# Each K and V load of a decode kernel issued as two transfers of 64 partitions

## The chip, the cores and the metric

The kernel runs on one core of one Trainium2 chip. The metric is the device time of one execution in microseconds; lower is better. The core has five engines that matter here: TensorE (PE in the profile, with its weight loads shown apart as PEld), VectorE (DVE), ScalarE (ACT), GpSimd (POOL) and SyncE (SP). SP computes nothing in this kernel: it issues every DMA. The profile counts sixteen DMA engines, which carry the data of all loads from HBM into SBUF.

## The reference

Four sequences, one token each, go through attention and a SwiGLU feed-forward layer, twice, with the same weights and the same K and V cache both times:

```python
B, Sq, D = 4, 1, 448
Hq, Hkv, Sk, Dh = 16, 8, 8192, 256
W = min(4096, max(256, Sk // 4))                     # 2048
q = (x @ wq).reshape(B, Sq, Hq, Dh).transpose(0, 2, 1, 3)
k = jnp.repeat(k_cache[:, :, Sk - W:, :], 2, axis=1)
v = jnp.repeat(v_cache[:, :, Sk - W:, :], 2, axis=1)
p = softmax(einsum("bhqd,bhkd->bhqk", q, k) * Dh ** -0.5)
A = einsum("bhqk,bhkd->bhqd", p, v).transpose(0, 2, 1, 3).reshape(B, Sq, Hq * Dh) @ wo
Bf = (silu(x @ w_gate) * (x @ w_up)) @ w_down
x = x + A(layernorm(x)); x = x + Bf(layernorm(x))    # twice over
```

Everything is bfloat16. The window of one sequence and one K/V head is 2048 rows of 256 values, so 1 MB of K and 1 MB of V. There are 4 x 8 such pairs in a layer.

## The kernel before, in words

**The unit of work is a pair**, one sequence t and one K/V head. For each pair the window of K is loaded as two transfers of 512 KB (line 609), the window of V as two more (line 626). Each goes into one buffer `half<i>` of 128 partitions x 4 KB; there are 15 such buffers (`NPOOL`). Each partition of a K load gets one run of 4096 bytes from HBM; each partition of a V load gets two runs of 2048 bytes.

**What uses a load.** A K load waits for one VectorE transposition (line 617), which writes it into one of six `KT` buffers and so frees the `half` buffer. Two of them make the pair's K ready for 32 matmuls that make the scores (line 637). Then come the row maximum, the exponentials on ScalarE (line 656), a rearrangement, and two groups of eight matmuls with V (line 677), one group for each V load. A V buffer is free when its group is done. After that the pair's two heads are normalised, flipped, and go through the output projection (line 724) with the weights in `wo_sb`.

**What is loaded once.** The weights (`wq_sb`, `wo_sb`, `wg_sb`, `wu_sb`, `wd_sb`, by line 389) are loaded once. Of each sequence the last five heads of K (transposed) and of V are kept from the first layer for the second (`KEEP_K`, `KEEP_V`). So 64 pairs are computed, and 44 of them load K and V: 88 loads of each.

**The order.** The program first builds a graph of operations with ranks, then a planner (`Graph.schedule`) lays the operations out on five queues by rank and by estimated times, and takes for each K or V load the buffer that is free first. What comes out is one fixed order for each engine. All DMAs stand in SP's order. A load that reuses a buffer waits on SP for the last reader of that buffer; whatever stands behind it on SP waits too. Each buffer has its own semaphore, `h<i>`. A load adds 16 to it when it has landed, and its readers wait for the count (`Graph._count`, `Graph.emit`).

**The planner's estimates of a load** are its bytes and the length of its runs (`o.nbytes`, `o.run`), not the number of DMA instructions.

Of the kernel before, what the change touches and what calls it, by code (L numbers as in the profile page):

```python
# [32 lines left out]
KLEAD = 2.2  # L33
VLAG = 1.3
# [20 lines left out]

class Op:
    __slots__ = ("i", "eng", "dur", "rank", "emit", "deps", "succ", "nbytes", "dsem", "dval",
                 "start", "end", "pos", "waits", "inc", "val", "known", "run", "cell", "rel")

    def __init__(self, i, eng, dur, rank, emit):  # L60
        self.i, self.eng, self.dur, self.rank, self.emit = i, eng, dur, rank, emit
        self.deps = {}
        self.succ = []
        self.nbytes = 0
        self.dsem = None
        self.dval = 0
        self.cell = None
        self.rel = ()
        self.inc = False
        self.val = 0  # L70
        self.waits = []


class Graph:
# [12 lines left out]
    def op(self, eng, dur, rank, emit, r=(), w=(), bank=(), acc=()):  # L87

        o = Op(len(self.ops), eng, dur, rank, emit)
        self.ops.append(o)  # L90
        for k in r:
            d = self.writer.get(k)
            if d is not None:
                self._dep(o, d, d.eng != eng or eng != PE)
        for k in tuple(w) + tuple(acc):
            for d in self.readers.get(k, ()):
                self._dep(o, d, d.eng != eng or eng != PE)
            d = self.writer.get(k)
            if d is not None:
                self._dep(o, d, d.eng != eng or eng != PE)  # L100
        for b in bank:
            last = self.banks.setdefault(b, {})
            for e, d in last.items():
                if e != eng:
                    self._dep(o, d, True)
            last[eng] = o
        for k in r:
            self.readers.setdefault(k, []).append(o)
        for k in tuple(w) + tuple(acc):
            self.writer[k] = o  # L110
            self.readers[k] = []
        return o

    def dma(self, rank, nbytes, emit, sem, r=(), w=(), run=8192, cell=None):

        o = self.op(SP, 0.05, rank, emit, r=r, w=w)
        o.run = run
        o.nbytes = nbytes
        o.cell = cell
        if cell is None:  # L120
            self._count(o, sem)
        return o

    def _count(self, o, sem):
        o.dsem = sem
        self.dcount[sem] = self.dcount.get(sem, 0) + 16
        o.dval = self.dcount[sem]


# [98 lines left out]
    def emit(self, eng_name, eng, sems, dsems):  # L228
        for o in self.order[eng_name]:
            for d in o.waits:  # L230
                if d.dsem is not None:
                    eng.wait_ge(dsems[d.dsem], d.dval)
                else:
                    eng.wait_ge(sems[d.eng], d.val)
            ins = o.emit(eng)
            if o.dsem is not None:
                ins.then_inc(dsems[o.dsem], 16)
            elif o.inc:
                ins.then_inc(sems[eng_name], 1)

# [38 lines left out]
def build(nc, A_x, A_k_cache, A_v_cache, A_wq, A_wo, B_x, B_w_gate, B_w_up, B_w_down, out):  # L279
    s0 = A_k_cache.shape[2] - WIN  # L280
    g = Graph()

    with ExitStack() as es:
        def sb(name, shape, dt):
            return es.enter_context(nc.sbuf_tensor(name, shape, dt))
# [6 lines left out]
        half = [sb(f"half{s}", [128, 8 * DH], BF16) for s in range(NPOOL)]  # L292
# [70 lines left out]
        for a in range(4):  # L363
            g.op(DVE, 0.1, R0, lambda e, a=a: e.memset(qmask[32 * a:32 * a + 32, a:a + 1], DH ** -0.5), r=("qmask",),
                 w=(f"qmask{a}",))
        g.op(DVE, 0.2, R0, lambda e: e.tensor_copy(
            permb[:, :].rearrange("p (r l) -> p r l", l=4), identb[:, :].rearrange("p (l r) -> p r l", l=4)),
            r=("identb",), w=("permb",))
        for a in range(4):
# [5 lines left out]
            w=("osel",))  # L375
        g.op(DVE, 0.2, R0, lambda e: e.tensor_reduce(lomask[:, :], iv[:, :, 1, :], AX.XY, ALU.add), r=("identb",),
             w=("lomask",))
# [199 lines left out]
        def x_in(e):  # L577
            last = None
            for cc in range(4):
# [6 lines left out]
             r=("z",), w=tuple(f"x{t}" for t in range(B)), bank=("Z",))  # L586
# [11 lines left out]
        pos = -1  # L598

        def pair(pos, si, side, nside, t, layer, kvh):  # L600
            p_, s_, q_ = pos % NY, pos % NS, pos % NQ
            if layer == 1 and (t, kvh) in kt_held:
                ks = kt_held.pop((t, kvh))
            else:
                ks = kt_free.pop(0)
                ksrc = A_k_cache[t, kvh, s0:s0 + WIN, :].rearrange("(p j) d -> p (j d)", p=128)
                for hf in range(2):
                    cell = []
                    g.dma(pos - KLEAD, 1 << 19, lambda e, cell=cell, hf=hf: e.dma_start(  # L609
                        half[cell[0]][:, :], ksrc[:, 2048 * hf:2048 * hf + 2048]), None, w=(f"k{pos}_{hf}",), run=4096,  # L610
                        cell=cell)
                    for q in range(TRP):
                        def tr(e, cell=cell, hf=hf, q=q):
                            n = 2 // TRP
                            src = half[cell[0]][:, :].bitcast(UINT32).rearrange("p (l k s) -> p l k s", l=2, k=16)
                            dst = KT[ks][:, :].bitcast(UINT32).rearrange("p (k l r) -> p l k r", k=16, l=4)
                            return e.transpose(dst[:, 2 * hf + q * n:2 * hf + q * n + n], src[:, q * n:q * n + n])  # L617
                        o = g.op(DVE, 1.12 / TRP + 0.06, pos, tr, r=(f"k{pos}_{hf}",), w=(f"kt{ks}_{hf}_{q}",))
                    o.rel = (cell,)
            if layer == 1 and (t, kvh) in v_held:  # L620
                vs = v_held.pop((t, kvh))
            else:
                vsrc = A_v_cache[t, kvh, s0:s0 + WIN, :].rearrange("(a q g) d -> q a g d", a=4, q=128)
                vs = [[], []]
                for hv, cell in enumerate(vs):
                    g.dma(pos + VLAG, 1 << 19, lambda e, cell=cell, hv=hv: e.dma_start(  # L626
                        half[cell[0]][:, :].rearrange("p (a g d) -> p a g d", a=2, g=4),
                        vsrc[:, 2 * hv:2 * hv + 2, :, :]), None, w=(f"v{t}_{kvh}_{hv}",), run=2048, cell=cell)
            at = first[t].index(kvh)
            keep_k, keep_v = (layer == 0 and at >= HKV - k for k in (KEEP_K, KEEP_V))  # L630

            def scores(e):
# [11 lines left out]
                r=(f"qc{t}_{kvh}",) + tuple(f"qmask{a}" for a in range(4)), w=(f"qe{q_}",))  # L644
# [3 lines left out]
                r=(f"s{s_}",), w=(f"pmax{s_}",), bank=(f"S{s_}",))  # L648
# [5 lines left out]
                r=(f"m{s_}",), w=(f"negm{s_}",), bank=(f"S{s_}",))  # L654
            for n in range(2):
# [3 lines left out]
                    r=(f"s{s_}", f"negm{s_}"), w=(f"praw{s_}_{n}",), bank=(f"S{s_}",))  # L659
            g.op(PE, 0.03, pos, lambda e: e.matmul(Yb[p_][:, 64:96], lhsT=permb[:, :], rhs=praw[s_][:, :], start=True,  # L660
                                                   stop=False, skip_group_check=True),
                 r=(f"praw{s_}_0", f"praw{s_}_1", "permb"), w=(f"yp{p_}",), bank=(f"Y{p_}",))
            g.op(PE, 0.03, pos, lambda e: e.matmul(Yb[p_][:, 32:64], lhsT=onesb[:, :], rhs=praw[s_][:, :], start=False,  # L663
                                                   stop=False, skip_group_check=True),
                 r=(f"praw{s_}_0", f"praw{s_}_1", "onesb"), w=(f"ysum{p_}",), bank=(f"Y{p_}",))
# [5 lines left out]
                r=(f"ysum{p_}",), w=(f"rs{p_}",), bank=(f"Y{p_}",))  # L671

            def pv(e, hv):
                last = None
                for a in range(2):
                    for gg in range(4):
                        last = e.matmul(Yb[p_][32 * gg:32 * gg + 4, 256:512],  # L677
                                        lhsT=pT[p_][:, 4 * gg + 2 * hv + a, :, :].rearrange("p y n -> p (y n)"),
                                        rhs=half[vs[hv][0]][:, 1024 * a + 256 * gg:1024 * a + 256 * gg + 256], start=False, stop=False, skip_group_check=True)
                return last  # L680
            for hv in range(2):
                kw = dict(acc=(f"y{p_}",)) if hv else dict(w=(f"y{p_}",))
                o = g.op(PE, 0.385, pos, lambda e, hv=hv: pv(e, hv), r=(f"pT{p_}", f"v{t}_{kvh}_{hv}"),
                         bank=(f"Y{p_}",), **kw)
                if not keep_v:
# [4 lines left out]
                 w=(f"oh{p_}",), bank=(f"Y{p_}",))  # L690
# [4 lines left out]
            def flip(e):  # L695
# [9 lines left out]
                r=(f"yo{p_}", f"ri{p_}"), w=(f"oT{si % 2}_{side}",), bank=(f"Y{p_}",))  # L705
# [26 lines left out]
        for si, pairs in enumerate(steps()):  # L732
# [8 lines left out]
            for t, layer in full:  # L741
                pos_ = pos
                pos = pos_ - CROSS
# [12 lines left out]
                pos = pos_  # L756
# [5 lines left out]
        dsems = {d: es.enter_context(nc.semaphore(f"d_{d}")) for d in g.dcount}  # L762
# [60 lines left out]
```

## Time and profile before

| | before |
|---|---|
| three runs | 323.88, 326.10, 326.27 us; median 326.1 us |
| profiled execution, from first to last instruction (span) | 322.9 us |
| what the median has beyond that span | 3.2 us |
| moved by DMA | 105.27 MB, mean 326 GB/s |
| busy: PE / DVE / POOL / ACT | 72% / 60% / 26% / 22% |
| K and V loads | 88 + 88, 512 KB each |
| granted TensorE clock | 1.000 |

The profile has no time of its own for the profiled execution beside its span; the runs lie 1.0 to 3.4 us above that span.

How to read it. A row of the groups of instructions names the line of the kernel, the engine, the operation and the tiles (output, then inputs), the shape and the count; then the busy time and the mean of one, and the idle time of that engine just before, with what ended most of it. A row of the chain of waits is one piece of the work that ended last: its start, its length, and what it was. A "DMA" piece there runs from the issue of a transfer to its landing. SPq rows are DMA instructions on SP's queue; a long one was held up at the queue. In a table of windows, each row gives for a stretch of time the busy time of each engine (with the number of instructions), the granted clock, the mean busy share of the sixteen DMA engines, and the rate in GB/s. The share is made from packet times and can come out a few per cent over 1.

### The profile page before, as it was taken

The page shows a single profiled execution, that of the slowest core. Times are in us where ns is not written, and L with a number is a line of the kernel's source. Part 1 is how long each engine was busy: PE and PEld are TensorE (multiplying, and loading weights), DVE is VectorE, ACT ScalarE, POOL GpSimd, SP SyncE. Part 2 cuts the span into 40 slices and gives each one's busy share as a digit, 9 for nine tenths or more (in the row PEclk, how much of TensorE's full clock was granted, in tenths as well). Part 3 has the DMA queues.
Part 4 walks back from the last instruction along what each step waited for, and adds up shares of the span by engine and source line. Part 5 has one row for each costly group of instructions (what it writes and reads, how often), then busy time and mean ns, then how long its engine had stood idle before and what let it go on. Part 6 is the DMA issues. An engine that isn't in the chain of part 4 may idle for free.

```text
span 322.9 us, 12873 instructions
## 1 busy us (share of the span) xinstructions
PE 232.6 (72%) x5728; PEld 169.7 (53%) x5728; DVE 192.6 (60%) x608; ACT 72.4 (22%) x289; POOL 84.9 (26%) x199
## 2 busy tenths in 40 slices
PE   3654454446588788578796895679787959889875
PEld 2542322234476465366664653567555636686554
DVE  5386555652145778765447787855377874656332
ACT  1112111111022333211231322113223322123310
POOL 3312111112023223240233331313233413134221
DMA  7999999999999999999889999999899999748000
GB/s 277 399 407 392 393 396 397 391 396 397 391 362 308 338 368 346 400 362 309 301 272 373 375 351 405 355 365 339 277 359 377 357 386 391 277 140 305 5 0 5
DMA packets 42327, 105.27 MB, mean 326 GB/s; under 512 B 3096, under 2 KB 7200, under 8 KB 41888
## 3 DMA queue, kind: packets, MB, share of 16 engines
q1 hardware_dynamic: 42272, 104.45, 88.0%
q8 instruction: 45, 0.74, 0.9%
q14 instruction: 10, 0.08, 0.1%
HBM read 104.44 MB, written 0.00 MB: 323 GB/s over the span
## 4 chain that ended last, share of the span: by engine, by line
DMA 38%; PE 34%; DVE 12%; SPq 7%; issue 5%; ACT 2%; POOL 0%; DVEq 0%
DMA half<-in_A_k_cache_dram 20%; DMA half<-in_A_v_cache_dram 12%; PE Y L677 11%; PE S L637 8%; DVE KT L617 6%; DMA wd_sb<-in_B_w_down_dram 5%; PE Z L473 4%; SPq L389 4%; PE A L724 3%; PE Z L514 3%; DVE oh L691 2%; PE Z L542 2%; SPq L609 2%; DVE small L652 2%; SPq L626 1%
## 5 line engine op out<-in xcount | busy, mean ns | idle before, releaser
L617 DVE STREAM_TRANSPOSE KT<-half 128x1024 uint32<-128x1024 uint32 x88 | 108.3, 1233 | 13.3 <-DMA half<-in_A_k_cache_dram 12.9
L637 PE MATMUL S<-qe,KT 128*128 128x8 bf16 x2048 | 64.6, 168 | 22.4 <-DVE KT L617 18.5
L677 PE MATMUL Y<-half,pT 128*4 128x256 bf16 x1024 | 70.0, 403 | 9.6 <-DMA half<-in_A_v_cache_dram 8.7
L637 PEld LDWEIGHTS S<-qe,KT 128*128 128x128 bf16 x2048 | 59.7, 104 | 30.7 <-DVE KT L617 20.8
L687 POOL TENSOR_TENSOR small<-small 128x2 f32<-128x2 f32 x64 | 44.3, 696 | 113.5 <-DVE small L669 103.3
L656 ACT ACTIVATE praw<-S,small 128x16 bf16<-128x16 f32 x128 | 28.7, 279 | 84.6 <-DVE small L652 83.9
L691 DVE SCALAR_TENSOR_TENSOR oh<-oh,small,Y 128x256 bf16<-128x256 bf16 x64 | 30.1, 472 | 23.9 <-ACT oh L689 23.4
L689 ACT ACTIVATE oh<-Y 128x256 bf16<-128x256 f32 x64 | 24.6, 384 | 74.2 <-PE Y L677 74.2
L641 POOL TENSOR_TENSOR qe<-qc,qmask 128x64 bf16<-128x64 bf16 x64 | 18.6, 294 | 71.3 <-PE S L637 52.3
L677 PEld LDWEIGHTS Y<-half,pT 128*4 128x4 bf16 x1024 | 20.0, 94 | 21.8 <-DMA half<-in_A_v_cache_dram 11.5
L646 DVE TRANSPOSE_TENSOR_REDUCE pmax<-S 128x1 bf16<-128x32 f32 x64 | 13.4, 211 | 27.1 <-PE S L637 25.3
L724 PE MATMUL A<-oT,wo_sb 128*128 128x1 bf16 (+1 forms) x688 | 24.8, 166 | 6.4 <-DVE oT L702 6.1
L724 PEld LDWEIGHTS A<-oT,wo_sb 128*128 128x128 bf16 x688 | 22.2, 105 | 10.5 <-DVE oT L702 8.5
L697 PE MATMUL Y<-osel,oh 128*128 128x2 bf16 x128 | 13.3, 173 | 17.4 <-DVE oh L691 17.2
L652 DVE TENSOR_REDUCE small<-S 128x2 f32<-128x128 f32 x64 | 17.4, 282 | 10.4 <-PE S L649 8.3
L666 ACT ACTIVATE pT<-Y 128x64 bf16<-128x64 f32 x64 | 14.1, 222 | 40.7 <-PE Y L663 40.4
L697 PEld LDWEIGHTS Y<-osel,oh 128*128 128x128 bf16 x128 | 8.8, 111 | 27.0 <-DVE oh L691 24.5
L649 PE MATMUL S<-identb,pmax 128*128 128x128 bf16 x64 | 16.6, 284 | 4.5 <-DVE pmax L646 3.6
L473 PE MATMUL Z<-xn,wq_sb 128*128 128x1 bf16 (+1 forms) x480 | 15.6, 165 | 2.6 <-DMA wq_sb<-in_A_wq_dram 1.9
L473 PEld LDWEIGHTS Z<-xn,wq_sb 128*128 128x128 bf16 x480 | 14.3, 104 | 3.4 <-DMA wq_sb<-in_A_wq_dram 2.0
L669 DVE TENSOR_REDUCE small<-Y 128x2 f32<-128x32 f32 x64 | 11.0, 177 | 7.1 <-ACT pT L666 6.8
L440 POOL TENSOR_SCALAR st<-st 128x1 f32<-128x1 f32 x16 | 4.3, 267 | 41.2 <-DVE st L428 40.7
(76 smaller groups left out, 212.0 us busy)
## 6 DMA issues: line engine op xcount, KB each, us to landing
half<-in_A_k_cache_dram SPq DMA_DIRECT2D x88, 512.0 KB, 7.0
half<-in_A_v_cache_dram SPq DMA_DIRECT2D x88, 512.0 KB, 6.7
wo_sb<-in_A_wo_dram SPq DMA_DIRECT2D x8, 448.0 KB, 12.3
wq_sb<-in_A_wq_dram SPq DMA_DIRECT2D x3, 1024.0 KB, 6.9
wd_sb<-in_B_w_down_dram SPq DMA_DIRECT2D x1, 1568.0 KB, 16.3
wg_sb<-in_B_w_gate_dram SPq DMA_DIRECT2D x1, 1344.0 KB, 14.2
wu_sb<-in_B_w_up_dram SPq DMA_DIRECT2D x1, 1344.0 KB, 14.7
wq_sb<-in_A_wq_dram SPq DMA_DIRECT2D x1, 512.0 KB, 10.4
```

The lines of the kernel that those rows point to most:

```text
L473: last = e.matmul(o, lhsT=lhsT, rhs=rhs, start=(cc == 0 and hh == 0 and ee == 0), stop=(cc == 3), skip_group_check=True)
L617: return e.transpose(dst[:, 2 * hf + q * n:2 * hf + q * n + n], src[:, q * n:q * n + n])
L637: last = e.matmul(Sb[s_][:, 8 * gg:8 * gg + 8], lhsT=kt[:, gg, ce // 2, ce % 2, :], rhs=qe[q_][:, ce, :, :], start=(gg == 0 and ce == 0), ...
L641: g.op(POOL, 0.25, pos - SLEAD - 1, lambda e: e.tensor_tensor(qe[q_][:, :, :, :], qc[t][:, kvh, :, :].unsqueeze(2).broadcast_to([128, 8, 4 ...
L652: g.op(DVE, 0.2, pos, lambda e: e.tensor_reduce(negm[s_][:, :], Sb[s_][:, 128:256].rearrange("p (k n) -> p n k", n=2), AX.X, ALU.max, nega ...
L656: g.op(SCA, 0.17, pos, lambda e, n=n: e.activation(praw[s_][:, :].rearrange("p (k n) -> p n k", n=2)[:, n, :], Sb[s_][:, 0:32].rearrange(" ...
L677: last = e.matmul(Yb[p_][32 * gg:32 * gg + 4, 256:512], lhsT=pT[p_][:, 4 * gg + 2 * hv + a, :, :].rearrange("p y n -> p (y n)"), rhs=half[ ...
L687: g.op(POOL, 0.25, pos, lambda e: e.tensor_tensor(ri[p_][:, :], rs[p_][:, :], expo[:, 1:3], op=ALU.pow), r=(f"rs{p_}", "expo"), w=(f"ri{p_ ...
L689: g.op(SCA, 0.28, pos, lambda e: e.activation(oh[p_][:, :], Yb[p_][:, 256:512], ACT.Copy), r=(f"y{p_}",), w=(f"oh{p_}",), bank=(f"Y{p_}",))
L691: g.op(DVE, 0.4, pos, lambda e: e.scalar_tensor_tensor(out=oh[p_][:, :], in0=oh[p_][:, :], scalar=lomask[:, 0:1], in1=Yb[p_][:, 256:512], ...
L697: last = e.matmul(Yb[p_][:, 2 * dh:2 * dh + 2], lhsT=oh[p_][:, :].rearrange("p (m e) -> p e m", e=2)[:, dh, :], rhs=osel[:, :], start=Fals ...
L724: last = e.matmul(Av[:, cc, sl], lhsT=wo_sb[:, 4 * kvh + k, c0:c0 + 128], rhs=oT[si % 2][:, k % 2, k // 2, 0:n], start=False, stop=False, ...
```

## The change

Each load of K or V is issued as two DMA instructions, one for partitions 0 to 63 and one for partitions 64 to 127, one right behind the other. Source, destination, runs and bytes are the same in sum. The load's readers wait until both have landed: the buffer's semaphore now counts 32 for a load in place of 16 (`parts=2`). The planner sees a load as one operation with the same numbers as before. The loads of weights, the input and the output are as they were.

```diff
-    def dma(self, rank, nbytes, emit, sem, r=(), w=(), run=8192, cell=None):
+    def dma(self, rank, nbytes, emit, sem, r=(), w=(), run=8192, cell=None, parts=1):
 
         o = self.op(SP, 0.05, rank, emit, r=r, w=w)
-        o.run = run
+        o.run, o.parts = run, parts
...
-        self.dcount[sem] = self.dcount.get(sem, 0) + 16
+        self.dcount[sem] = self.dcount.get(sem, 0) + 16 * o.parts
...
             if o.dsem is not None:
-                ins.then_inc(dsems[o.dsem], 16)
+                for i in ins if o.parts > 1 else (ins,):
+                    i.then_inc(dsems[o.dsem], 16)
...
-                    g.dma(pos - KLEAD, 1 << 19, lambda e, cell=cell, hf=hf: e.dma_start(
-                        half[cell[0]][:, :], ksrc[:, 2048 * hf:2048 * hf + 2048]), None, w=(f"k{pos}_{hf}",), run=4096,
-                        cell=cell)
+                    g.dma(pos - KLEAD, 1 << 19, lambda e, cell=cell, hf=hf: [e.dma_start(
+                        half[cell[0]][c:c + 64, :], ksrc[c:c + 64, 2048 * hf:2048 * hf + 2048]) for c in (0, 64)],
+                        None, w=(f"k{pos}_{hf}",), run=4096, cell=cell, parts=2)
...
-                    g.dma(pos + VLAG, 1 << 19, lambda e, cell=cell, hv=hv: e.dma_start(
-                        half[cell[0]][:, :].rearrange("p (a g d) -> p a g d", a=2, g=4),
-                        vsrc[:, 2 * hv:2 * hv + 2, :, :]), None, w=(f"v{t}_{kvh}_{hv}",), run=2048, cell=cell)
+                    g.dma(pos + VLAG, 1 << 19, lambda e, cell=cell, hv=hv: [e.dma_start(
+                        half[cell[0]][c:c + 64, :].rearrange("p (a g d) -> p a g d", a=2, g=4),
+                        vsrc[c:c + 64, 2 * hv:2 * hv + 2, :, :]) for c in (0, 64)],
+                        None, w=(f"v{t}_{kvh}_{hv}",), run=2048, cell=cell, parts=2)
```

How this stands in SP's order, just before and at the place where loads first wait for a buffer (a row is a line of the program, the target and the source, partitions x elements, the engine whose semaphore it waits for, and how often it repeats; `half` is a K/V buffer, `wo_sb` the output projection's weights). Before:

```order
L389 DMA wo_sb<-in_A_wo_dram 128x2x896
L609 DMA half<-in_A_k_cache_dram 128x2048
L609 DMA half<-in_A_k_cache_dram 128x2048 [waits s_dve]
L626 DMA half<-in_A_v_cache_dram 128x2x1024 [waits s_dve] x2
L389 DMA wo_sb<-in_A_wo_dram 128x2x896
```

Now, with the lines of the changed kernel:

```order
L390 DMA wo_sb<-in_A_wo_dram 128x2x896
L610 DMA half<-in_A_k_cache_dram 64x2048 x2
L610 DMA half<-in_A_k_cache_dram 64x2048 [waits s_dve]
L610 DMA half<-in_A_k_cache_dram 64x2048
L627 DMA half<-in_A_v_cache_dram 64x2x1024 [waits s_dve]
L627 DMA half<-in_A_v_cache_dram 64x2x1024
```

Each load has become two instructions next to each other; the wait for the buffer stands on the first alone, and no load has changed its place among the others. The orders of PE, DVE, ACT and POOL are the same instruction for instruction, as are the waits on PE and DVE.

And the last loads of SP's order. Before:

```order
L609 DMA half<-in_A_k_cache_dram 128x2048 [waits s_pe] x4
L609 DMA half<-in_A_k_cache_dram 128x2048 [waits s_dve]
L609 DMA half<-in_A_k_cache_dram 128x2048 [waits s_pe]
L626 DMA half<-in_A_v_cache_dram 128x2x1024 [waits s_dve] x4
L626 DMA half<-in_A_v_cache_dram 128x2x1024 [waits s_pe] x2
L573 DMA out_dram<-KT 4x448 [waits s_dve]
```

Now, the last four V transfers and what stands behind them:

```order
L627 DMA half<-in_A_v_cache_dram 64x2x1024 [waits s_pe]
L627 DMA half<-in_A_v_cache_dram 64x2x1024
L627 DMA half<-in_A_v_cache_dram 64x2x1024 [waits s_pe]
L627 DMA half<-in_A_v_cache_dram 64x2x1024
L574 DMA out_dram<-KT 4x448 [waits s_dve]
```

The stream of loads ends as before with two V loads, each now in two pieces, and behind them only the store of the output.

More of the change, by code (lines that the diff above doesn't have):

```diff
@@ L57 @@
     __slots__ = ("i", "eng", "dur", "rank", "emit", "deps", "succ", "nbytes", "dsem", "dval",
-                 "start", "end", "pos", "waits", "inc", "val", "known", "run", "cell", "rel")
+                 "start", "end", "pos", "waits", "inc", "val", "known", "run", "parts", "cell", "rel")
     def __init__(self, i, eng, dur, rank, emit):
```

## The prediction

> **What bounds the kernel now.** I read the busy shares first, then the rate of DMA by stretches, then the chain of waits, then the queue of SP. The page's busy shares name no compute engine as the bound, and the DMA queue's row does:
>
> ```profile
> PE 232.6 (72%) x5728; PEld 169.7 (53%) x5728; DVE 192.6 (60%) x608; ACT 72.4 (22%) x289; POOL 84.9 (26%) x199
> ...
> q1 hardware_dynamic: 42272, 104.45, 88.0%
> ```
>
> PE, the busiest, is idle for 28% of the span, while the sixteen DMA engines are busy for 88% of it with the 104.45 MB of the loads. An average hides stages, so I cut the span into stretches (each row: length, busy time of the engines, the granted clock, DMA share, GB/s):
>
> ```profile
> 0.00:8.00 8.00, 2.46 (x14) 1.95 (x14) 4.58 (x49) 1.27 (x1) 3.04 (x13) 1.00 0.72 274
> 8.00:20.00 12.00, 7.02 (x195) 6.23 (x195) 5.99 (x16) 1.55 (x9) 3.46 (x11) 1.00 1.01 403
> 20.00:60.00 40.00, 19.89 (x457) 13.03 (x461) 24.83 (x52) 7.04 (x29) 7.60 (x15) 1.00 1.04 395
> 60.00:88.00 28.00, 14.95 (x357) 10.48 (x349) 10.42 (x35) 3.26 (x13) 4.03 (x9) 1.00 1.05 395
> 88.00:120.00 32.00, 26.45 (x678) 19.82 (x679) 20.04 (x55) 8.66 (x34) 7.96 (x19) 1.00 0.95 344
> 120.00:200.00 80.00, 62.12 (x1522) 44.12 (x1518) 55.11 (x162) 20.64 (x84) 24.29 (x54) 1.00 0.96 349
> 200.00:290.00 90.00, 74.44 (x1876) 54.97 (x1877) 58.55 (x192) 22.62 (x91) 26.01 (x61) 1.00 0.92 331
> 290.00:300.00 10.00, 9.40 (x243) 6.91 (x240) 6.06 (x21) 3.32 (x13) 4.12 (x10) 1.00 0.76 260
> 300.00:322.90 22.90, 15.90 (x404) 12.18 (x403) 7.02 (x35) 3.99 (x16) 4.43 (x9) 1.00 0.01 3
> ```
>
> Three stages. From 8 to 88 us the DMA engines are full (share 1.01 to 1.05) and the rate stands at 395 to 403 GB/s; PE is busy half the time or less. From 88 to 300 us they are nearly full, at 260 to 349 GB/s. From 300 us nothing is loaded and PE finishes. The chain says the same: in the first stage it runs from load to load, later through loads and matmuls in turn, and at the end through PE alone.
>
> ```profile
> 31.35 12.03 DMA half<-in_A_k_cache_dram
> ...
> 110.33 7.01 DMA half<-in_A_k_cache_dram
> ...
> 257.91 8.90 DMA half<-in_A_v_cache_dram
> ...
> 308.67 1.41 PE Y L677 x24
> ```
>
> A load takes 12 us to land in the first stage and 7 to 9 later, though 512 KB (524,288 bytes) at 395 GB/s are moved in 1.33 us: it mostly stands in line behind others. So anything that changes the rate of the stream changes the time, and anything that only lengthens one load's own way is partly hidden in that line.
>
> **The part that adds instructions.** Issues on SP go from 88 + 88 to 176 + 176:
>
> ```profile
> L609 SPq DMA_DIRECT2D half<-in_A_k_cache_dram x88: 327/388/2530, 3.3 to 279.7; - x88
> ...
> L626 SPq DMA_DIRECT2D half<-in_A_v_cache_dram x88: 367/379/10296, 10.8 to 292.6; - x88
> ```
>
> The median issue is 0.38 to 0.39 us, so the 176 new ones are 176 x 0.38 = 67 us of SP. On SP they lie beside the transfers: two issues take 0.77 us, while the queue needs 1.33 us for the load even at full rate. The work that hides them is the earlier loads in line. If the line is empty, the second half starts 0.38 us late; ten legs of the chain after 110 us are loads, so at most ten times 0.38 = 4 us. I take nothing, and keep 4 us for a rival. The readers' wait costs no instruction: it is the same wait with a higher count. Splitting by partitions gives no reader an earlier start, since the transposition of a K load and the eight matmuls of a V load still wait for both halves. No wait is new, and what stands behind a waiting issue on SP is the same loads as before. On the other engines nothing moves.
>
> **The part that changes the transfers.** Now a transfer reaches 64 partitions in place of 128; if its work is still dealt to all sixteen engines, each carries 4 partitions in place of 8. The runs, and so the pieces that an engine moves, stay as they were. What this does to the rate is the whole question, and no row shows a transfer of some size to 64 partitions. What the rows do show is that the full rate does not depend on what is read: it is 395 in the stretch that loads mostly K and V (runs of 4096 and 2048 bytes), and 395 in the stretch with the feed-forward weights, whose `wd` has runs of 896 bytes. It is not set by HBM's row length, nor by an engine of compute. The ceiling is at something that all these loads have in common: either the sixteen DMA engines (395 / 16 = 24.7 GB/s each) or the way into the 128 partitions (395 / 128 = 3.09 GB/s each). All of them spread over all 128 partitions, and so the trace cannot separate the two by itself.
>
> If it is the engines, the rate stays. If it is the way into the partitions, a transfer to one half can have 64 x 3.09 = 197 GB/s. Whether the two halves then add up depends on when they are carried. If every engine takes its pieces in the order of SP's queue, each does first half A of a load, then half B, then A of the next. Two engines that share one way in and are in step both need A's way, then both B's, and each gets half: the K and V data take twice their time. Two engines that are apart by just one half (0.66 us) never meet, and it takes once. At random distances the mean is 1.5 times. A load has landed only when its slowest engine has, and the queue cannot run far ahead of it, so the stream goes by the pairs that meet most. I therefore take the middle between 1.5 and 2, 1.75, and keep both ends.
>
> [...]
>
> **The sum.** K and V are 176 x 524,288 bytes = 92.27 MB, at 395 GB/s 233.6 us. The rest of the 104.45 MB is 12.18 MB, 30.8 us, unchanged. The first 8 us moved 274 GB/s x 8 us, which is 5.5 us at 395: 2.5 us are lost before the stream runs. Together 267 us with no wait in the stream. After the last load today come 22.9 us, of which PE still works off a backlog; only from about 308.7 us (the last matmuls with V) to the end, 14.2 us, is the chain that must follow the last load. With a slower stream the backlog is gone: a pair that loads needs four loads, 4 x 1.33 x 1.75 = 9.3 us, and PE has 232.6 / 64 = 3.6 us for a pair. I take 16 us, near the lower bound. Today's waits in the stream, 212 us from 88 to 300 for 71.3 MB that need 181 us at 395, are 31 us, and go, since buffers are now free before their turn.
>
> The profiled span is 322.9 us, and the median of the runs 326.1, so 3.2 us are added at the end. With f for the factor on K and V: 2.5 + 30.8 + 233.6 f + 16 + 3.2 = 52.5 + 233.6 f. For f = 1.75 it is 461 us; for 1.5, 403; for 2, 520. Up to f = 1.17 the 31 us of waits and the shorter end would pay for it. What is late next is only the stream itself: K for the transpositions, V for line 677.
>
> **The rivals.**
>
> *The engines are the ceiling, and nothing happens.* For it speaks that the share is full at 1.01 to 1.05 in the very stretches with 395 GB/s: the engines look busy, not blocked. Against it, if a packet that is held up at its destination counts as busy too, the share says nothing of where it is held up, and no row parts the two. Sixteen engines still carry each transfer, 24.7 GB/s each, the issues are hidden: 326 us, 324 to 329. This decides if engines never wait for a partition's way in. Chance 0.11.
>
> *It gets faster.* Place: 88 to 300 us, where the rate is 260 to 349 GB/s because loads wait for buffers:
>
> ```profile
> SPq L609 <- PE Y L677: 25.0, 17, 3.8
> ```
>
> That is SP's wait for the matmuls that free a V buffer. If pieces half as long let the engines fill the gaps after such a wait (each engine has 4 partitions of a load to finish before it can begin another piece, not 8), and the ceiling is the engines, the 31 us of waits are what can be won at most: 295 us. It decides where the rate of this stretch comes up towards 395. Against it: a buffer is released as late as before, and gaps behind waits are not filled by cutting what comes after them. Half of it, 310 us, is the value I give this case. Chance 0.05.
>
> *The rate stays, but the second issue shows.* Where the line is empty, ten legs of 0.38 us: 330 us. Against it, even a late load takes 7 us against 1.33 of transfer. Chance 0.03.
>
> *The ways in do matter, but engines fall out of step and stay so* (one engine that runs ahead by half a load meets nobody). Then f is 1.17 to 1.5: 326 to 403 us, about 365. For it: nothing in the queue forces them into step, and all loads are queued some 12 us deep in the first stage. Against it: nothing pushes them apart, and a load waits for all. Chance 0.11.
>
> *Forecast, f from 1.5 to 2.* 403 to 520 us. Chance 0.70: no row counts against it, and the common spread over 128 partitions, which every full-rate row of the trace has, is the one thing that the change takes away.
>
> **The numbers.** The predicted time is 461 us. The range goes from 335 us (into the partly out of step case, most of which it holds) to 525 (f = 2 with 5 us more at the end, still under today's 22.9): it leaves out the first three rivals, 0.19, and little else. The forecast's own range is 403 to 520. Some 1% is what the runs can tell from no change. Faster by over 1% is 0.05; within 1% is 0.11; slower by over 1% is 0.03 + 0.11 + 0.70 = 0.84.
>
> **What would show it.** If the forecast holds, the windows from 20 to 60 us and from 120 to 200 us show a DMA share near 1 with a rate between 200 and 290 GB/s, while the stretch of the feed-forward weights, whose transfers still have 128 partitions, goes faster than its neighbours. The landing time of a load in line goes from 12 us towards 21. The chain of waits is loads almost to the end, the waits of SP for L677 shrink, and what follows the last load is 14 to 18 us long. If the stream is at 395 in the first stage as before, the step from 128 to 64 partitions was wrong altogether, and 461 with it; then the count of SP's issues and the stretch after 88 us decide between the first three rivals. If the share falls well below 1 while the rate falls, the issues were not hidden. A rate of 300 to 350 in the first stage means that the engines fell out of step.

## The result and the profile after

| | before | after |
|---|---|---|
| median of the runs | 326.09 us (323.88 to 326.27) | 435.62 us (426.98 to 446.87) |
| ratio, 95% interval | | 1.324, 1.313 to 1.335 |
| profiled execution: span, its own time | 322.9 us | 430.7 us, 432.5 us |

The medians are from all runs, the ratio from the undisturbed ones alone (after: 426.98 and 432.52 us; the two others, 438.72 and 446.87 us, were slow). The kernel is a third slower, by 101 and 106 us in the two. The busy times of the engines are nearly the same; what changed is the time that the DMA engines need. The page after, busy shares and the queue of SP:

```profile
PE 235.4 (55%) x5728; PEld 169.2 (39%) x5728; DVE 195.0 (45%) x608; ACT 73.0 (17%) x289; POOL 85.1 (20%) x199
...
q1 hardware_dynamic: 45088, 104.46, 96.0%
```

The same 104.46 MB fill the sixteen engines for 96% of a span that is 108 us longer. By stretches (length, busy times, granted clock, DMA share, GB/s):

```profile
0.00:8.00 8.00, 2.46 (x14) 1.95 (x14) 4.58 (x49) 1.28 (x1) 3.05 (x13) 1.00 0.72 276
8.00:20.00 12.00, 5.25 (x146) 4.74 (x146) 3.08 (x9) 1.54 (x9) 3.16 (x10) 1.00 1.03 288
20.00:60.00 40.00, 12.98 (x304) 8.85 (x304) 17.67 (x39) 4.41 (x18) 5.24 (x11) 1.00 1.05 236
60.00:88.00 28.00, 7.96 (x166) 4.67 (x166) 9.41 (x18) 2.90 (x11) 2.40 (x5) 1.00 1.05 238
88.00:120.00 32.00, 12.17 (x267) 8.00 (x267) 10.87 (x29) 3.32 (x13) 4.30 (x10) 1.00 1.05 282
120.00:200.00 80.00, 50.57 (x1290) 37.54 (x1294) 40.63 (x115) 15.47 (x62) 16.79 (x38) 1.00 1.04 293
200.00:290.00 90.00, 50.42 (x1192) 34.50 (x1184) 45.07 (x131) 16.53 (x67) 18.80 (x43) 1.00 1.04 249
...
380.00:400.00 20.00, 13.18 (x356) 11.19 (x355) 11.31 (x40) 3.12 (x13) 6.08 (x17) 1.00 0.75 185
400.00:415.00 15.00, 11.70 (x298) 8.53 (x296) 5.35 (x24) 4.90 (x22) 3.02 (x5) 1.00 0.53 121
415.00:430.70 15.70, 10.18 (x264) 8.17 (x264) 4.32 (x24) 1.63 (x7) 3.05 (x7) 1.00 0.01 2
```

From 20 to 88 us the engines are as full as before (1.05) and move 236 to 238 GB/s in place of 395. The stretch from 88 us, with the transfers of the feed-forward weights, which still have 128 partitions, is faster (282), and so is what comes after it (293), before it falls back to 249. The chain of waits now runs from load to load for longer, each landing after some 18 us in place of 12 in the first stage; at the end stand the same matmuls as before:

```profile
31.99 17.63 DMA half<-in_A_v_cache_dram
...
53.25 18.21 DMA half<-in_A_v_cache_dram
...
416.54 1.41 PE Y L679 x24
```

The waits after, who waited for whom (total, times, longest):

```profile
DVE KT L618 <- DMA half<-in_A_k_cache_dram: 73.6, 53, 6.7
...
PE Y L679 <- DMA half<-in_A_v_cache_dram: 49.8, 35, 3.4
```

The waits for K were 12.9 us and those for V on PE 8.7 us before. SP's waits for the matmuls with V, which free V buffers, went the other way: from 25.0 to 15.7 us ahead of K loads and from 19.5 to 7.7 us ahead of V loads. Engines that used to make the loads wait now wait for the data.

### The profile page after: what moved, and what is told of

It is laid out like the page before. It is cut to its first block, busy times and chain, and to the rows that moved or that the text cites. A ratio compares the mean times of both kernels' runs of the same rounds, so it can differ in the third digit from the quotient of the medians.

```text
span 430.7 us, 13049 instructions
## 1 busy us (share of the span) xinstructions
PE 235.4 (55%) x5728; PEld 169.2 (39%) x5728; DVE 195.0 (45%) x608; ACT 73.0 (17%) x289; POOL 85.1 (20%) x199
## 3 DMA queue, kind: packets, MB, share of 16 engines
q1 hardware_dynamic: 45088, 104.46, 96.0%
## 4 chain that ended last, share of the span: by engine, by line
DMA 51%; PE 20%; SPq 12%; DVE 7%; issue 7%; ACT 1%; POOL 0%; DVEq 0%
DMA half<-in_A_v_cache_dram 31%; DMA half<-in_A_k_cache_dram 20%; SPq L627 7%; PE Y L679 6%; SPq L610 5%; PE S L639 4%; DVE KT L618 3%; PE Z L474 3%; PE Z L515 2%; PE A L726 1%; DVE oh L693 1%; SPq L390 1%; PE Z L543 1%; DVE small L654 1%; ACT oh L691 1%
## 5 line engine op out<-in xcount | busy, mean ns | idle before, releaser
L679 PE MATMUL Y<-half,pT 128*4 128x256 bf16 x1024 | 71.0, 402 | 56.8 <-DMA half<-in_A_v_cache_dram 49.8
L671 DVE TENSOR_REDUCE small<-Y 128x2 f32<-128x32 f32 x64 | 10.9, 176 | 12.9 <-ACT pT L668 12.6
L651 PEld LDWEIGHTS S<-identb,pmax 128*128 128x128 bf16 x64 | 6.3, 107 | 26.2 <-DVE pmax L648 20.2
## 6 DMA issues: line engine op xcount, KB each, us to landing
wd_sb<-in_B_w_down_dram SPq DMA_DIRECT2D x1, 1568.0 KB, 19.5
```

The source lines that it names most:

```text
L651: g.op(PE, 0.1, pos, lambda e: e.matmul(Sb[s_][:, 128:256], lhsT=pmax[s_][:, 0:1].broadcast_to([128, 128]), rhs=identb[:, :], start=True, ...
L679: last = e.matmul(Yb[p_][32 * gg:32 * gg + 4, 256:512], lhsT=pT[p_][:, 4 * gg + 2 * hv + a, :, :].rearrange("p y n -> p (y n)"), rhs=half[ ...
```

## The experiments

Two theories stood at the start. **Theory 1:** the rate depends on which partitions a transfer reaches, as if partitions 0 to 63 shared a narrower way in and 64 to 127 another. **Theory 2:** the loss comes from twice as many transfers of half the size.

### Cut by columns in place of partitions

```diff
-    half[cell[0]][c:c + 64, :], ksrc[c:c + 64, 2048 * hf:2048 * hf + 2048]) for c in (0, 64)],
+    half[cell[0]][:, c:c + 1024], ksrc[:, 2048 * hf + c:2048 * hf + c + 1024]) for c in (0, 1024)],
...
-    half[cell[0]][c:c + 64, :].rearrange("p (a g d) -> p a g d", a=2, g=4),
-    vsrc[c:c + 64, 2 * hv:2 * hv + 2, :, :]) for c in (0, 64)],
+    half[cell[0]][:, 1024 * c:1024 * c + 1024].rearrange("p (g d) -> p g d", g=4),
+    vsrc[:, 2 * hv + c, :, :]) for c in (0, 1)],
```

> The changed kernel with each K and V load cut in two by columns in place of partitions: two transfers of 256 KB, 128 partitions each, the same number of instructions, the same waits and order (the K runs become 2048 bytes long). Theory 1, the way into 64 partitions is narrower: the loss goes, 324 to 335 us, and the stretch from 20 to 60 us moves about 390 GB/s again. Theory 2, the loss comes from twice as many transfers of half the size: it stays as in the changed kernel, 427 to 447 us, some 236 GB/s in that stretch.

Measured: 331.24 us, ratio to before 1.016 (1.006 to 1.027). The windows of this kernel:

```profile
20.00:60.00 40.00, 18.77 (x421) 12.00 (x421) 24.58 (x51) 7.04 (x29) 7.58 (x15) 1.00 1.05 385
```

That is 385 GB/s with 352 transfers of 256 KB. Theory 2 falls: number and size cost 1.6% together with the shorter K runs, not 32%.

### Even and odd partitions in place of lower and upper

```diff
-    half[cell[0]][c:c + 64, :], ksrc[c:c + 64, 2048 * hf:2048 * hf + 2048]) for c in (0, 64)],
+    half[cell[0]][c:128:2, :], ksrc[c:128:2, 2048 * hf:2048 * hf + 2048]) for c in (0, 1)],
```

The V transfers are cut in the same way.

> The changed kernel with the even and the odd partitions of each K and V load as its two transfers, in place of the lower and the upper 64: the same number of transfers, the same 64 partitions each, the same runs, waits and order. Theory 1 (which partitions a transfer reaches sets the rate): the whole loss goes, 324 to 335 us. If the count of transfers, their issue or the doubled count in the semaphores cost anything in this kernel beyond that, it shows here as the rest: the run cut by columns was 1.6% slower than before, so some 5 us are possible.

Measured: 328.58 us, ratio 1.009 (1.004 to 1.014). Its windows:

```profile
20.00:60.00 40.00, 19.78 (x456) 12.74 (x453) 24.41 (x49) 7.02 (x29) 7.58 (x15) 1.00 1.05 394
...
88.00:300.00 212.00, 167.68 (x4180) 121.63 (x4180) 137.64 (x418) 53.33 (x216) 60.59 (x140) 1.00 0.93 330
```

This is the changed kernel in everything but which 64 partitions belong together, and the loss is gone: 394 GB/s in the first stage. What is left of it, 0.9% or some 3 us, is what splitting as such costs in this kernel. It does not lie in the first stage, where the line of loads is deep (395 GB/s before), but after it: 330 GB/s from 88 to 300 us, where before has 336:

```profile
88.00:300.00 212.00, 172.41 (x4307) 125.82 (x4308) 139.76 (x426) 55.24 (x222) 62.38 (x143) 1.00 0.93 336
```

### Loads alone: whole, halves, lower half only

These kernels hold nothing but SP's loads into 15 buffers in turn, with the transfers themselves written as in the full kernels (the loop in short; each of these kernels ran once):

```diff
+    if cnt[s]:
+        e.wait_ge(sems[s], cnt[s])
+    for dp, sp in lst:        # whole: all; halves: 0-63, then 64-127; lower: 0-63 alone
+        mv(dp, sp).then_inc(sems[s], 16)
+        cnt[s] += 16
```

> Loads alone: the 176 K and V loads of 512 KB to 128 partitions, into 15 buffers in turn, each waiting only for the load before it in the same buffer. All computation and all weights are left out. 92.27 MB at the 395 GB/s of the first stage of before are 234 us; both theories expect 235 to 245 us.

> Loads alone as in the run above, each load as two transfers of 64 partitions, lower then upper. Computation and weights left out. Both theories expect the rate of the changed kernel's first stage, about 236 GB/s, so about 391 us (350 to 470: theory 1 lets it lie anywhere from 1.5 to 2 times the time of whole loads, by how far the engines are out of step).

> Loads alone, only the lower 64 partitions of each load: 176 transfers of 256 KB, 46.1 MB, nothing to partitions 64 to 127. Computation and weights left out. Theory 1: no transfer finds the other half to fall out of step into, so the rate is the full half, about 197 GB/s, 234 us, lower in rate than with both halves. Theory 2 (a cost for each transfer): half of the time of both halves, about 195 us or the same 236 GB/s. If 64 partitions cost nothing by themselves: 117 us at 395 GB/s.

Measured: 240.1, 398.8 and 227.3 us. The windows (length, busy time of POOL, clock, DMA share, GB/s), whole loads first:

```profile
100.00:200.00 100.00, 0.00 (x0) 1.00 1.04 398
```

Lower and upper halves:

```profile
20.00:60.00 40.00, 0.00 (x0) 1.00 1.05 236
100.00:200.00 100.00, 0.00 (x0) 1.00 1.05 237
```

The lower half alone:

```profile
100.00:200.00 100.00, 0.00 (x0) 1.00 1.05 210
```

So 236 GB/s in the changed kernel's first stage is the rate of the loads by themselves; nothing in the computation makes it. Transfers to partitions 0 to 63 alone get 210 GB/s, where the prediction had worked out 197. And alternating halves get only 12 to 13% more than that.

The busy share stands near 1.05 at all three rates, because the packets of a slower stream are each under way for longer. By the packet records of the three traces, a packet of K, one run of 4096 bytes, takes a median of 164 ns with whole loads, 294 with halves and 315 with the lower half alone. So a packet that is held up counts as busy, which the prediction's first rival had left open.

### Even and odd partitions, loads alone

> Loads alone, each as two transfers of 64 partitions, but the even and the odd partitions in place of the lower and the upper 64. Computation and weights left out. Theory 1 (it matters which partitions a transfer reaches: 0 to 63 share half of the ways in): each transfer now reaches all of them, so the rate is above 236 GB/s, up to 398, 240 to 320 us. If the bare count of 64 partitions costs the rate: 236 GB/s again, 399 us.

Measured: 243.2 us. Its windows:

```profile
100.00:200.00 100.00, 0.00 (x0) 1.00 1.04 398
```

This is the full rate of whole loads, with 64 partitions in each transfer. The count of 64 in place of 128 costs nothing here (398 GB/s with both); which 64 they are does. This pair of runs decides it: 398 against 237 GB/s, with the same number of transfers, partitions, bytes and runs; the full kernels say the same in the first stage, 394 against 236.

One thing the runs do not part: which partitions a transfer reaches also fixes which rows it reads from HBM. Against a limit on the side of the source speaks that K and V are held up alike, though the lower half of a K load reads 4 KB out of every 8 KB over 512 KB, and that of a V load two solid stretches of 128 KB. With the lower half alone a packet of K takes 315 ns in place of 164, one of V 166 in place of 86 (medians).

### Are the engines in step?

In the prediction's model two engines share a way, which no run shows. If they only meet because they are in step, putting half of the engines back by one half should undo it; and half as many changes between the halves should halve whatever the changes win.

```diff
+    for i in range(2):
+        e.dma_start(side[0:8, 4096 * i:4096 * i + 4096], A_wq[0:8, :]).then_inc(sg, 16)
...
-    lst = [(lo, lo), (hi, hi)]
+    lst = [(lo, lo), (hi, hi)] if n % 2 else [(hi, hi), (lo, lo)]
```

(The first part is the run that was to put engines back, the second the run with alternating order; both are written out with the values that the kernels' settings give.)

> Loads alone in halves, lower then upper, with one thing ahead of them: two transfers of 64 KB to 8 partitions, which, if they go to eight of the sixteen engines, put these behind the other eight by 16 KB each, the time of one half (0.64 us). Computation and weights left out. Theory 1a (two engines that share a way meet because they are in step, and nothing pulls them together again): engines of a pair now take turns, the rate goes to 350 to 398 GB/s, 240 to 270 us. Theory 1b (the order in which the engines meet is set again by the queue, or both engines of a pair were put back alike): 236 GB/s as without, 399 us.

> Loads alone in halves, one load lower then upper, the next upper then lower, so that two transfers to the same half follow one another. Computation and weights left out. Theory 1 with engines that meet in part (now 1.68 times the time of whole loads, so they are apart by some of a half): with twice as long a stretch in each half the same distance relieves half as much, 1.84 times, about 215 GB/s, 430 us. If the alternation itself costs (a price for each change of half, of which there are now half as many): faster than 399 us, about 320 us.

Measured: 409.4 and 422.8 us. The windows of the run with the two small transfers ahead:

```profile
100.00:200.00 100.00, 0.00 (x0) 1.00 1.05 231
```

And of the run with alternating order:

```profile
100.00:200.00 100.00, 0.00 (x0) 1.00 1.05 222
```

The small transfers did not make the engines take turns: 231 GB/s, a little worse than without. The packet records show why: the distance was never made. A packet of K has 4096 bytes and one of V 2048, and at almost any time some sixteen packets are under way (a share of 1.05 to 1.06 of the sixteen engines), which I take as one for each engine. The small transfers do go eight packets at a time, but the last of these ends at 3.3 us, while the first packets of K start on all sixteen engines between 3.15 and 3.6 us. At the first turn from K to V, near 8 us, the number of packets of V among the sixteen goes from two to fourteen within 0.44 us, as it does without the small transfers (0.4 to 0.7 us at all 44 turns); eight engines that were behind by one half would need 0.64 us or more (16 KB, four packets of K at the 0.16 us of whole loads). So this run does not test whether engines that take turns get the full rate.

The alternating order came out near its expectation. A half of 262,144 bytes takes 1.25 us at 210 GB/s, 1.11 us at 236 with a change after every half, and 1.18 us at 222 with a change after every second: some 0.14 us gained for a change in both cases. That fits engines that are nearly in step, with a small gain at each change that does not depend on how long the stretches are: a turn from K to V takes 0.44 us in the middle, where a half takes 1.11. The gain itself is an estimate, worked out from one run each.

### Two queues

Lower halves by SP, upper halves by ScalarE:

```diff
+        @block.scalar
+        def _(e):
+            stream(e, slice(64, 128))
...
+            cnt = stream(e, slice(0, 64))
```

> Loads alone in halves, the lower halves issued by SP and the upper halves by ScalarE, each on its own queue. Computation and weights left out. In one queue the engines meet because both halves come to every engine in the same order; each change of half won 0.14 us (half after half 236 GB/s, with half as many changes 222, with none 210). If an engine takes pieces of both queues in turn, the changes come with every piece (0.16 us at full rate) and the rate is near 398 GB/s, 240 us. If each engine works off one transfer before it turns to the other queue, it is 236 GB/s as with one queue, 399 us.

Measured: 296.2 us. Its windows:

```profile
100.00:200.00 100.00, 0.00 (x0) 1.00 1.05 322
```

This lies between the two expectations. Halves from two queues overlap much better than from one (322 against 237), so a good part of the loss comes from both halves standing in one queue's order; but they still lose 19% against whole loads. How an engine takes turns between two queues, no row here shows.

### K alone, V alone

In the first kernel only K is in halves, in the second only V (the edit shown is the first's; the second does the same to the K loads):

```diff
-    g.dma(pos + VLAG, 1 << 19, lambda e, cell=cell, hv=hv: [e.dma_start(
-        half[cell[0]][c:c + 64, :].rearrange("p (a g d) -> p a g d", a=2, g=4),
-        vsrc[c:c + 64, 2 * hv:2 * hv + 2, :, :]) for c in (0, 64)],
-        None, w=(f"v{t}_{kvh}_{hv}",), run=2048, cell=cell, parts=2)
+    g.dma(pos + VLAG, 1 << 19, lambda e, cell=cell, hv=hv: e.dma_start(
+        half[cell[0]][:, :].rearrange("p (a g d) -> p a g d", a=2, g=4),
+        vsrc[:, 2 * hv:2 * hv + 2, :, :]),
+        None, w=(f"v{t}_{kvh}_{hv}",), run=2048, cell=cell)
```

> The changed kernel with the K loads in halves of 64 partitions and the V loads whole. If the loss is carried by each load in halves by itself: by the prediction's sum with 1.64 (from 435.6 us) for K alone, 52.5 + 116.8 x 1.64 + 116.8 = 361 us, 345 to 375. If it were the waits for buffers or SP's issues that grow, K alone would show nearly nothing (326 to 331 us) or the whole (420 us or more).

> The changed kernel with the V loads in halves of 64 partitions and the K loads whole. By the prediction's sum, a loss carried by each load for itself, 361 us. K alone showed 423 to 443 us, which says that halves also slow the whole loads next to them: then V alone is as slow too, 410 to 440 us.

> Loads alone, K in halves, V whole. Computation and weights left out. If each kind keeps the rate that it has alone (236 and 398 GB/s): 296 GB/s together, 317 us. If whole loads in between put the engines of a pair in step, K goes at the 210 GB/s of the lower half alone: 275 GB/s, 340 us. If halves and whole loads also meet each other: less than 275 GB/s, over 340 us.

Measured: K alone 423.2 and 443.5 us, V alone 423.7 and 426.5 us, loads alone with K in halves 391.8 us. The windows of that last run:

```profile
20.00:60.00 40.00, 0.00 (x0) 1.00 1.05 260
100.00:200.00 100.00, 0.00 (x0) 1.00 1.05 243
300.00:350.00 50.00, 0.00 (x0) 1.00 1.05 230
```

Half of the loads in halves cost nearly as much as all of them, in the full kernel (at the least 423.2 and 423.7 against 427.0 us) and in the stream (391.8 against 398.8). K alone at over 420 us is also what its expectation gave to growing waits or issues; the stream by itself, which has no computation to wait for, rules out the waits, and SP's issues for a pair, 2.46 us for the four of K and 1.10 for the two of V at the start of its queue, fill 3.6 of the 8.9 us that a pair takes there (391.8 / 44). The mixed stream begins at 260 GB/s, well under the 296 that the two kinds would give by themselves, and sinks to 230 within 300 us. Whole loads next to halves lose their own rate: a packet of V, whole here, takes a median of 145 ns in this stream, 84 to 87 where all loads are whole. In the changed kernel's first stage the packets of `wo_sb`, whole as before, take 131 ns in place of 78. As the rate sinks, the engines do get further apart: the turn from K to V takes 0.7 us at first, 3.2 us near 80 us, and by 300 us there is no time at which all sixteen carry the same kind. Whether the rate sinks because of this was not tried.

## Why the prediction was right, point by point

**What bounds the kernel:** right. The stream of loads, not an engine, set the time before and after; its rate fell and PE's busy time stayed (232.6 to 235.4 us). One reading was loose: by the chain before, the ten loads after 110 us landed in 4.9 to 8.9 us, not 7 to 9.

**The part that adds instructions:** right that it hides in the first stage (394 GB/s with even and odd partitions), and about right in price where the line is short. The forecast took nothing and kept 4 us for a rival; the run with even and odd partitions shows 0.9% (0.4 to 1.4%), about 3 us. One term was too small: an issue to 64 partitions took longer here than one to 128. The K loads of the changed kernel:

```profile
L610 SPq DMA_DIRECT2D half<-in_A_k_cache_dram x176: 465/597/3240, 3.3 to 384.2; - x176
```

The median is 0.60 us in place of 0.39.

**Engines or the way into the partitions:** decided for the partitions, with the reservation on the source above. The common spread over all 128 partitions was the thing taken away, and the even and odd run gives it back with the same transfers otherwise: 398 GB/s with loads alone, 394 in the first stage of the full kernel. The 197 GB/s that the prediction worked out for one half came near: the lower half alone has 210 in a steady stream. A stream of both halves in one queue gained 12 to 13% on that, and from two queues 53% (322 against 210). That two engines share a way was the author's model; the runs show rates, not the ways that packets take.

**The factor f:** about the right size, in part by luck. The prediction took 1.75, the middle between the two ends of its model, engines at random distances (1.5) and engines in step (2); no run shows either end. In the first stage it is 395 / 236 = 1.67, with loads alone 398 / 236 = 1.69. The end for engines in step was too high: one half alone carries 210 of 398, so by the same model in step means 1.90. And with loads alone the engines are not at random distances: a turn from K to V takes 0.44 us where a half takes 1.11. What lowers 1.90 to 1.69 there is worked out as a gain of some 0.14 us at each change of half. But in the changed kernel, from 20 to 88 us, the turn takes 1.3 to 2.1 us (the packets of K among the sixteen going from fourteen to two), a fifth of the bytes are whole transfers of `wo_sb`, and the rate is 236 to 238 all the same. So what sets 1.67 stays open; no run set the distance between engines.

**Each load pays for itself:** wrong. The sum is linear in the bytes that are in halves, 52.5 + 233.6 f, and for half of these bytes it would give 361 us (with f = 1.64, from the median of 435.6). K alone and V alone each gave about 424. The sum came out near for the change as it was, because most of the bytes are K and V in halves; it would have failed for a part of it. Its term of 30.8 us for everything else, unchanged, goes by the same false step: the packets of `wo_sb` slowed down too (131 ns for 78).

**The stretch of the weights:** right against what comes before it, not against what comes after. The rate goes from 242 GB/s before 100 us to 305, and is 316 in the next window. The finer windows of the changed kernel:

```profile
100.00:120.00 20.00, 8.88 (x198) 6.01 (x198) 5.90 (x21) 2.26 (x9) 3.34 (x8) 1.00 1.04 305
120.00:140.00 20.00, 11.90 (x339) 9.88 (x340) 5.32 (x19) 1.98 (x7) 1.73 (x5) 1.00 1.07 316
...
200.00:220.00 20.00, 12.10 (x343) 9.34 (x336) 8.43 (x25) 3.17 (x12) 2.63 (x7) 1.00 1.05 248
```

The last packet of the weights ends at 125.5 us, and from 130 to 140 us the halves by themselves have 321 GB/s. So for some 80 us after the weights the halves lose less, sinking to 248 GB/s; from 120 to 200 us the rate is 293, just over the 290 that the forecast allowed. SP held the queue for 11.3 us just before (waiting for `xe`), so the line of loads was all but empty there (no packet of K or V from 112.4 to 123.0 us); why the halves then lose less is not shown. The prediction had f constant; over the whole stream it averages 1.61 (below).

**The end:** too short. The prediction took 16 us after the last load, with PE's backlog gone. SP's last V loads, and where they end:

```profile
384.82 17.33 SPq L627 DMA_DIRECT2D half<-in_A_v_cache_dram  x12
```

The last issue ends at 402.2 us and, by the packet records, the last packet of V at 408.7, so 22 us follow, where the forecast allowed 14 to 18. The chain from the last matmuls with V to the end is 14.2 us as before (416.5 to 430.7), but a backlog of some 8 us stands ahead of it. The stream also had gaps again from 380 us, 185 GB/s at a share of 0.75. That the waits for buffers go was right for the long middle (share 1.04 to 1.05), not for the end.

**The sum with what was measured:** 2.5 + 30.8 + 233.6 f + 22 = 430.7 gives f = 1.61. Against the forecast of 461 us that is 33 us less for f (1.61 for 1.75), 6 more for the end and 1.4 less for what lies around the span (1.8 for 3.2): some 432.6 us, beside the profiled execution's 432.5. That it closes proves nothing, since f is solved for here; it also holds the time that the weights lost and the gaps after 380 us. The forecast's 461 was too long mainly by f, and two errors of opposite sign, f and the end, cancelled in part.

**The rivals:** the three with an unchanged rate fall, by 236 against 395 GB/s. The one in which engines fall out of step and stay so is seen in part and for a time, after the weights (321 GB/s is f = 1.23), not as a state that lasts.

## What to carry to other kernels

In this case a transfer's partitions mattered by which they were, not by how many: partitions 0 to 63 by themselves got about half of the full rate into SBUF, 210 of 398 GB/s (64 to 127 by themselves were not run), the even 64 and the odd 64 in turn got all of it (398), and cutting a load into the lower and upper half on one queue did not add the halves up (237). Where a load must be cut, cut it by columns or by even and odd partitions, which cost 1 to 2% here. In a kernel whose DMA engines are full, look at the rate in GB/s of a full stretch, not at the busy share: it stood at 1.05 at 395 and at 236 GB/s alike.

## What the runs showed that was not expected

- Half of the loads in halves cost nearly as much as all: at the least 423.2 us for K alone, 423.7 for V alone and 427.0 for both; with loads alone 391.8 and 398.8 us.
- The time of an issue on SP went by the shape of its target: a median of 0.38 to 0.39 us for 512 KB to 128 partitions in the kernel before (0.43 and 0.47 us beside loads in halves), 0.43 us for 256 KB to 128 partitions by columns, 0.60 to 0.62 us for 256 KB to 64 partitions in the full kernels, whether lower and upper or even and odd (0.49 us for K with the lower half alone).
- Two queues, each with its own half, move 322 GB/s where one queue with both moves 237, though the busy share of the engines is 1.05 in both.
- A rate that differs by about the same time at each change of half: 0.14 us, with a change after every half and after every second.
- Whole loads were slowed by halves next to them (145 ns for a packet of V in place of 84 to 87), and in a stream that mixed both the sixteen engines drifted apart, from 0.7 us at a turn from K to V to over 3 us after 80 us.
